# Cosine attention and a GELU layer on one core: q and k prepared over four slots, idle matmuls in the first batch

## Chip, cores and metric

One Trainium2 chip, one of its cores. The metric is the device time of one execution in microseconds (us), the median of several runs. Engines are named as in the profile: PE (TensorE, matmuls; PEld is its loading of weights), DVE (VectorE), ACT (ScalarE), POOL (GpSimd), SP (SyncE, here only a queue that issues DMAs).

## The reference

```python
# q, k, v: (8, 12, 448, 64); tau = 0.1
q_n = q / (norm(q, axis=-1) + 1e-06)
k_n = k / (norm(k, axis=-1) + 1e-06)
scores = q_n @ k_n.T / tau
attn = softmax(scores)
a = attn @ v                                   # (8, 12, 448, 64)
x = a.transpose(0, 2, 1, 3).reshape(8 * 448, 768)
h = x @ w_in                                   # w_in: (768, 2048)
g = 0.5 * h * (1 + erf(h / sqrt(2)))
out = g @ w_out                                # w_out: (2048, 768), out (3584, 768) f32
```

## The kernel before, in words

The 12 heads of a batch are taken as 6 pairs; the 48 pairs of all batches are numbered g = 0 to 47. For each pair the work is a row of steps, each a small function:

- `load_qk(g)` brings q and k of the pair (SP's queue, two DMAs), `load_v(g)` v (POOL's queue, cast to bf16).
- `square(g)` makes `sq` (1024 elements per partition) on POOL, `reduce(g)` the sums `nq` on DVE, `root(g)` the square root on ACT as Ln and Exp of half of it (`lq`, `sr`), `scale(g)` adds 1e-6 (`se`), takes the reciprocal (`rn`) on DVE and multiplies into `qkb`, q on POOL and k on DVE at the same time.
- `transposes(g)` puts `qkb` through PE into the bank `tp`, and DVE copies it out as `qkT`. `tp` shares its PSUM bank (tag "sm") with the sums `sm` of `values`.
- `scores(g, c0)` makes two of the four score tiles `st` on PE (two buffers) and their exponentials `pt` on ACT. The maximum isn't subtracted, since cosine scores are bounded.
- `values(g)` makes `sm` (sums of the exponentials, against ones) and `o` (against v) on PE, `normalise(g)` the reciprocal of the sums as Ln and Exp on ACT (`ln`, `rs`) and the product `x` on DVE.

`attention(b, fill)` runs a batch in six slots, one per pair. In slot g the kernel takes the scores of g, the values of g-1, the transposes of g+1 and the preparation of later pairs. Between them `run` puts in matmuls of `fill`: the second layer (`op`, 16 matmuls and a copy `ot` each) of the batches before, 96 of them in odd batches and 128 in even ones, none in batch 0. `first(b)` is the first layer of the batch (`hp`, 16 groups of 6 matmuls) with GELU on ACT (`g`); near its end it takes the transposes and the first half of the scores of the next batch's first pair. What is left of `op` comes at the end.

Each engine works its queue in the order in which the code is written (`manual_schedule`); an instruction that waits holds up what stands behind it. How far ahead a step runs is set by `upto(what, n, f)`, which calls f for all pairs up to n-1 that aren't done. The weights are loaded on POOL's queue (`wi` in 6 pieces, `wo` in 4), one or two per slot of batch 0.

The line numbers in the profile of before are those of the printed functions: `square` L103 to L106, `reduce` L113 and L115, `root` L121 and L123, `scale` L129 to L135, `transposes` L146 and L147, `scores` L157 and L160, `values` L170, `normalise` L178 to L181, `op` L196, `ot` L200, `hp` L289, GELU L293.

Of the kernel before, what the change touches and what calls it, by code (L numbers as in the profile page):

```python
# [8 lines left out]
F32 = mybir.dt.float32  # L9
BF16 = mybir.dt.bfloat16  # L10
AF = mybir.ActivationFunctionType
# [4 lines left out]
def kernel(  # L16
# [15 lines left out]
    nc = tc.nc  # L32
    B, H, S, D = q.shape
    NC = 4
    CS = S // NC
# [4 lines left out]
    KD = d_model // 128  # L40
# [3 lines left out]

    consts = ctx.enter_context(tc.tile_pool(name="consts", bufs=1))
    wpool = ctx.enter_context(tc.tile_pool(name="wpool", bufs=1))
    qkp = ctx.enter_context(tc.tile_pool(name="qkp", bufs=5))
    sqp = ctx.enter_context(tc.tile_pool(name="sqp", bufs=2))
    vp = ctx.enter_context(tc.tile_pool(name="vp", bufs=6))
    nrm = ctx.enter_context(tc.tile_pool(name="nrm", bufs=3))  # L50
    qkbp = ctx.enter_context(tc.tile_pool(name="qkbp", bufs=3))
# [8 lines left out]
    ps_mm = ctx.enter_context(tc.tile_pool(name="ps_mm", bufs=2, space=bass.MemoryType.PSUM))  # L60
# [3 lines left out]
    ident = consts.tile([CS, CS], BF16)  # L64
# [2 lines left out]
    nc.vector.memset(ones, 1.0)  # L67
    tiny = consts.tile([CS, 1], F32)
    nc.vector.memset(tiny, 1e-30)

    wi = wpool.tile([128, KD, d_ff], BF16, tag="wi")
    wo = wpool.tile([128, KF, d_model], BF16, tag="wo")
# [5 lines left out]
    x_t, g_t = {}, {}  # L78
# [19 lines left out]
    def square(g):  # L98
        sq = sqp.tile([CS, 2, 2, NC, D], F32, tag="sq", name=f"sq{g}")
        sq_t[g] = sq  # L100
        t = qk_t[g]
        if g == 0:
            nc.scalar.activation(sq[:, 1], t[:, 1], AF.Square)  # L103
            nc.vector.tensor_tensor(sq[:, 0], t[:, 0], t[:, 0], ALU.mult)
        else:
            nc.gpsimd.tensor_tensor(sq, t, t, ALU.mult)  # L106

# [32 lines left out]
    def transposes(g):  # L140
        qkb = qkb_t.pop(g)
        tp = ps_acc.tile([128, 2, NC, CS], BF16, tag="sm", name=f"tp{g}")
        qkT = qkTp.tile([128, 2, NC, CS], BF16, tag="qkT", name=f"qkT{g}")
        for i in (1, 0):
            for c in range(NC):
                nc.tensor.transpose(tp[:, i, c, :], qkb[:, i, c].rearrange("p h d -> p (h d)"), ident)  # L146
        nc.vector.tensor_copy(qkT, tp)  # L147
        qkT_t[g] = qkT


    def scores(g, c0):
        qkT = qkT_t[g]
        for c in (c0, c0 + 1):
            st = ps_st.tile([CS, 2, 512], F32, tag="st", name=f"st{g}_{c}")
            for h in range(2):
                rows = slice(h * D, (h + 1) * D)
                nc.tensor.matmul(st[:, h, :S], lhsT=qkT[rows, 1, c, :], rhs=qkT[rows, 0, :, :],  # L157
                                 start=True, stop=True)
            pt = ptp.tile([CS, 2, S], BF16, tag="pt", name=f"pt{g}_{c}")
            nc.scalar.activation(pt, st[:, :, :S], AF.Exp, scale=inv_tau)  # L160
            pt_t[g, c] = pt
# [65 lines left out]
    def upto(what, n, f):  # L227
        while done[what] < min(n, NG):
            f(done[what])
            done[what] += 1  # L230


    def attention(b, fill):
        fill = list(fill)

        def run(n):
            for _ in range(max(0, min(n, len(fill)))):
                fill.pop(0)()

        x_t[b] = xp.tile([128, HP, S], BF16, tag="x", name=f"x{b}")  # L240
        tail = 20 if fill else 0
        for i in range(HP):
            g = b * HP + i
            share = (len(fill) - tail) // (HP - i) if i else 30
            upto("red", g + 3 if g else 2, reduce)
            if g == 0 or i > 0:
                scores(g, 0)
            if i > 0:
                run(share // 3)
                upto("root", g + 3, root)  # L250
                values(g - 1)
                normalise(g - 1)
            else:
                run(24)
                upto("root", g + 3 if g else 2, root)
            if g == 0:
                upto("sc", 2, scale)
            scores(g, 2)
            if i < HP - 1:
                transposes(g + 1)  # L260
            if g == 0:
                upto("sq", 3, square)
                upto("red", 3, reduce)
                upto("root", 3, root)
            upto("sc", g + 3, scale)
            upto("sq", g + 4, square)
            upto("qk", g + 8, load_qk)
            upto("v", g + 4, load_v)
            for _ in range(2 if b == 0 and i < 4 else 1):
                if weights:  # L270
                    weights.pop(0)()
            run(share - share // 3 if i else 6)
        g = b * HP + HP - 1
        run(len(fill) - 8)
        values(g)
        normalise(g)
        run(len(fill))


    def first(b):  # L280
        sb, hf = divmod(b, 2)
        if hf == 0:
            g_t[sb] = gp.tile([128, KF, 2 * S], BF16, tag="g", name=f"g{sb}")
        nc.scalar.preload_act_table_set(GELU_SET)
        hps = {}

        def mm(m, kds):
            for kd in kds:
                nc.tensor.matmul(hps[m][:, :S], lhsT=wi[:, kd, m * 128:(m + 1) * 128],  # L289
                                 rhs=x_t[b][:, kd, :], start=(kd == 0), stop=(kd == KD - 1))  # L290

        def gelu(m):
            nc.scalar.activation(g_t[sb][:, m, hf * S:(hf + 1) * S], hps.pop(m)[:, :S], AF.Gelu)  # L293

        for m in range(KF):
            if m == KF - 5 and b + 1 < B:
                transposes((b + 1) * HP)
            if m != 1:
                hps[m] = ps_mm.tile([128, 512], F32, tag="mm", name=f"hp{b}_{m}")
            if m == 0:  # L300
                hps[1] = ps_mm.tile([128, 512], F32, tag="mm", name=f"hp{b}_1")
                mm(0, range(KD - 1))
                mm(1, range(KD - 1))
                mm(0, (KD - 1,))
            else:
                mm(m, (KD - 1,) if m == 1 else range(KD))
            gelu(m)
        if b + 1 < B:
            nc.scalar.preload_act_table_set(EXP_SET)
            scores((b + 1) * HP, 0)  # L310
# [1 line left out]

    upto("qk", 1, load_qk)
    nc.scalar.preload_act_table_set(EXP_SET)
    upto("qk", 5, load_qk)
    upto("v", 3, load_v)
    upto("sq", 1, square)
    upto("red", 1, reduce)
    upto("sq", 2, square)
    upto("root", 1, root)  # L320
    upto("sc", 1, scale)
    transposes(0)

    fill = []
    for b in range(B):
        attention(b, fill)
        first(b)
        sb, hf = divmod(b, 2)
        fill = [f for t in (range(3) if hf == 0 else range(3, 7)) for f in second_pieces(sb, t)]
# [37 lines left out]
```

## Time and profile before

| | |
|---|---|
| runs | 583.62, 584.01 and 586.18 us, median 584.01 |
| profiled execution | 584.36 us, of which the span of the profile is 582.6 |
| busy share of the span | PE 84%, ACT 56%, DVE 34%, POOL 34%, PEld 43% |
| granted TensorE clock, mean | 0.945 |
| moved by DMA | 45.35 MB |
| most expensive groups | `pt` on ACT 164.9 us (192), `op` 175.6 (896) and `hp` 150.0 (768) on PE |

Busy PE is modelled, since matmuls overlap in the pipeline; a share of 84% doesn't say that PE could do no more. In a row of the windows view stand the stretch (us from the start of the span), its length, for each engine the busy time and the instructions begun, the granted clock, the share of time that the 16 DMA engines were busy, and what they moved. In the chain of waits stand start, length, engine, tile and line: the work that ended last, followed back from the last instruction. In a row of the timeline the bracket gives the idle time of the engine ahead of the instruction, and what ended it.

### The profile page before, as it was taken

What the parts mean: (1) busy time and instruction counts of PE and PEld (TensorE: products, weight loads), DVE (VectorE), ACT (ScalarE), POOL (GpSimd) and SP (SyncE); (2) the same over time, 40 slices, a digit from 0 to 9 for tenths busy, and PEclk for the clock granted to TensorE, in tenths of its full rate; (3) what the DMA queues carried; (4) which work ended last, traced back from release to release, by engine and by line L of the source; (5) the groups of instructions that cost most, each with busy time, mean ns of one, the idle gap of its engine ahead of it and who ended that gap; (6) DMA issues with size and microseconds to landing.
All of it is one profiled execution on the core that took longest, in us unless ns stands there. A gap on an engine that the chain in (4) does not pass through costs nothing.

```text
span 582.6 us, 7930 instructions
## 1 busy us (share of the span) xinstructions
PE 492.1 (84%) x3200; PEld 248.1 (43%) x3200; DVE 195.6 (34%) x348; ACT 324.7 (56%) x529; POOL 196.3 (34%) x159
## 2 busy tenths in 40 slices
PE   2576997789987998779987999779988899869996
PEld 0233453345533454334543445334544455434453
DVE  4434114450255312443145412444124431453011
ACT  3465555664665546565565646556466655667410
POOL 4667305441144502543044420455025430440000
PEclk9996798899989999899998999789998899899999
DMA  8499903232044401324024420433114330110012
GB/s 213 105 199 200 198 2 100 58 96 67 3 104 108 121 13 40 92 64 125 1 68 106 107 66 1 107 79 104 31 37 101 80 97 1 37 16 28 28 27 82
DMA packets 42054, 45.35 MB, mean 78 GB/s; under 512 B 3361, under 2 KB 37665, under 8 KB 42017
## 3 DMA queue, kind: packets, MB, share of 16 engines
q1 hardware_dynamic: 27280, 32.81, 18.7%
q0 software_dynamic: 14496, 11.80, 14.3%
q8 instruction: 25, 0.41, 0.3%
q10 hardware_dynamic: 240, 0.23, 0.1%
q14 instruction: 13, 0.10, 0.1%
HBM read 45.61 MB, written 11.01 MB: 97 GB/s over the span
## 4 chain that ended last, share of the span: by engine, by line
PE 49%; POOL 20%; DVE 16%; ACT 9%; issue 4%; DMA 1%; POOLq 0%; SPq 0%
PE hp L289 25%; PE op L196 15%; POOL sq L106 12%; POOL qkb L135 9%; DVE nq L115 7%; DVE qkT L147 3%; DVE x L181 3%; PE tp L146 3%; ACT ln L178 3%; PE st L157 2%; ACT lq L121 2%; PE o L170 2%; ACT rs L180 2%; PE sm L170 2%; DVE rn L131 2%
## 5 line engine op out<-in xcount | busy, mean ns | idle before, releaser
L160 ACT ACTIVATE pt<-st 112x896 bf16<-112x896 f32 x192 | 164.9, 910 | 34.0 <-PE st L157 33.4
L135 POOL TENSOR_TENSOR qkb<-qk,rn 112x512 bf16<-112x512 f32 x48 | 70.3, 1464 | 324.4 <-DVE rn L131 284.7
L196 PE MATMUL op<-wo,g 128*128 128x384 bf16 x896 | 175.6, 346 | 0.0
L289 PE MATMUL hp<-x,wi 128*128 128x448 bf16 x768 | 150.0, 354 | 3.5 <-ACT g L293 3.5
L293 ACT ACTIVATE g<-hp 128x448 bf16<-128x448 f32 x128 | 68.8, 544 | 86.5 <-PE hp L289 86.5
L196 PEld LDWEIGHTS <-g 128*128 128x128 bf16 x896 | 85.2, 102 | 70.8 <-issue 28.2
L289 PEld LDWEIGHTS <-wi 128*128 128x128 bf16 x768 | 74.9, 98 | 74.6 <-issue 7.4
L115 DVE TENSOR_REDUCE nq<-sq 112x16 f32<-112x1024 f32 x47 | 57.3, 1218 | 103.3 <-POOL sq L106 103.3
L106 POOL TENSOR_TENSOR sq<-qk 112x1024 f32<-112x1024 f32 x47 | 88.6, 1885 | 2.8 <-DMA qk<-in_k_dram 2.8
L146 PE MATMUL tp<-ident,qkb 112*128 112x112 bf16 x384 | 30.1, 226 | 69.3 <-ACT ln L178 58.2
L157 PE MATMUL st<-qkT 64*112 64x448 bf16 x384 | 65.7, 413 | 9.1 <-DVE qkT L147 8.0
L121 ACT ACTIVATE lq<-nq,tiny 112x16 f32<-112x16 f32 x48 | 14.8, 308 | 96.8 <-DVE nq L115 95.7
L147 DVE COPY qkT<-tp 128x896 bf16<-128x896 bf16 x48 | 29.7, 618 | 106.4 <-PE tp L146 106.4
L200 DVE COPY ot<-op 128x384 f32<-128x384 f32 x56 | 31.0, 553 | 89.0 <-PE op L196 89.0
L146 PEld LDWEIGHTS <-qkb 112*128 112x128 bf16 x384 | 24.7, 103 | 84.7 <-issue 70.0
L170 PE MATMUL sm<-pt,ones 112*64 112x448 bf16 x384 | 53.2, 396 | 3.8 <-ACT pt L160 2.8
L181 DVE TENSOR_TENSOR x<-o,rs 128x448 bf16<-128x448 f32 x48 | 30.0, 625 | 73.4 <-ACT rs L180 48.5
L170 PE MATMUL o<-pt,v 112*64 112x448 bf16 x384 | 48.7, 379 | 0.0
L157 PEld LDWEIGHTS <-qkT 64*112 64x112 bf16 x384 | 22.2, 136 | 49.9 <-issue 28.0
L135 DVE TENSOR_TENSOR qkb<-qk,rn 112x512 bf16<-112x512 f32 x48 | 34.1, 710 | 1.8 <-DVE rn L131 0.2
L95 POOL DMA_DIRECT2D v<-in_v_dram x48 | 34.2, 712 | 0.2 <-issue 0.2
L170 PEld LDWEIGHTS <-ones 112*64 112x64 bf16 x384 | 19.8, 118 | 32.8 <-issue 27.0
(22 smaller groups left out, 139.1 us busy)
## 6 DMA issues: line engine op xcount, KB each, us to landing
qk<-in_q_dram SPq DMA_DIRECT2D x48, 224.0 KB, 2.8
qk<-in_k_dram SPq DMA_DIRECT2D x47, 224.0 KB, 3.0
v<-in_v_dram POOLq DMA_DIRECT2D x48, 112.0 KB, 3.0
wi<-in_moe_w_in_dram POOLq DMA_DIRECT2D x6, 512.0 KB, 6.7
wo<-in_moe_w_out_dram POOLq DMA_DIRECT2D x4, 768.0 KB, 11.7
out_dram<-ot SPq DMA_DIRECT2D x8, 336.0 KB, 2.9
out_dram<-ot SPq DMA_DIRECT2D x8, 288.0 KB, 2.6
out_dram<-ot SPq DMA_DIRECT2D x8, 240.0 KB, 3.1
```

Of the source, the lines that this page charges most:

```text
L106: nc.gpsimd.tensor_tensor(sq, t, t, ALU.mult)
L115: nc.vector.tensor_reduce(nq, sq, mybir.AxisListType.X, ALU.add)
L135: eng.tensor_tensor(qkb[:, i].rearrange("p c h d -> p h c d"), t[:, i], rn[:, i].to_broadcast([CS, 2, NC, D]), ALU.mult)
L146: nc.tensor.transpose(tp[:, i, c, :], qkb[:, i, c].rearrange("p h d -> p (h d)"), ident)
L147: nc.vector.tensor_copy(qkT, tp)
L157: nc.tensor.matmul(st[:, h, :S], lhsT=qkT[rows, 1, c, :], rhs=qkT[rows, 0, :, :], start=True, stop=True)
L160: nc.scalar.activation(pt, st[:, :, :S], AF.Exp, scale=inv_tau)
L170: nc.tensor.matmul(dst[h * D:(h + 1) * D, :S], lhsT=ones if dst is sm else v_t[g][:, h, c, :], rhs=pt_t[g, c][:, h, :], start=(c == 0), st ...
L181: nc.vector.tensor_tensor(x_t[b][:, p, :], o[:, :S], rs, ALU.mult)
L196: nc.tensor.matmul(ps[:, :NH], lhsT=g_t[sb][:, kf, t * 128:(t + 1) * 128], rhs=wo[:, kf, ni * NH:(ni + 1) * NH], start=(kf == 0), stop=(kf ...
L289: nc.tensor.matmul(hps[m][:, :S], lhsT=wi[:, kd, m * 128:(m + 1) * 128], rhs=x_t[b][:, kd, :], start=(kd == 0), stop=(kd == KD - 1))
L293: nc.scalar.activation(g_t[sb][:, m, hf * S:(hf + 1) * S], hps.pop(m)[:, :S], AF.Gelu)
```

## The change

The order of the preparation is changed, and with it the number of buffers. In slot g, POOL now squares pair g+4 (before: g+3) ahead of its multiplication of pair g+2 (before: behind it), DVE reduces pair g+3 (before: g+2), ACT takes the root of g+2 as before, and the scaling is of g+2 as before. q and k have 6 buffers instead of 5 and are loaded one pair earlier, `sq` has 3 instead of 2. Pair 1 is squared on ACT.

In batch 0 each call of `run` puts in four matmuls of zeros whose result nobody reads (`spin`), 56 in all, and 24 more stand ahead of the first transposes. In `first` the groups of `hp` are written one after another; before, groups 0 and 1 took their first five matmuls each, then their last ones.

```diff
-    qkp = ctx.enter_context(tc.tile_pool(name="qkp", bufs=5))
-    sqp = ctx.enter_context(tc.tile_pool(name="sqp", bufs=2))
+    qkp = ctx.enter_context(tc.tile_pool(name="qkp", bufs=6))
+    sqp = ctx.enter_context(tc.tile_pool(name="sqp", bufs=3))
...
+    blank = consts.tile([CS, S], BF16)
+    nc.vector.memset(blank, 0.0)
...
+        elif g == 1:
+            nc.scalar.activation(sq, t, AF.Square)
...
+    def spin(n):
+        ps = ps_mm.tile([128, 512], F32, tag="mm", name="spin")
+        for _ in range(n):
+            nc.tensor.matmul(ps[:CS, :S], lhsT=ident, rhs=blank, start=True, stop=True)
...
         def run(n):
+            if b == 0:
+                spin(4)
             for _ in range(max(0, min(n, len(fill)))):
                 fill.pop(0)()
...
-            upto("red", g + 3 if g else 2, reduce)
             if g == 0 or i > 0:
                 scores(g, 0)
+            upto("sq", g + 5, square)
+            upto("red", g + 4, reduce)
...
             scores(g, 2)
             if i < HP - 1:
                 transposes(g + 1)
-            if g == 0:
-                upto("sq", 3, square)
-                upto("red", 3, reduce)
-                upto("root", 3, root)
+            upto("root", g + 3, root)
             upto("sc", g + 3, scale)
-            upto("sq", g + 4, square)
-            upto("qk", g + 8, load_qk)
+            upto("qk", g + 9, load_qk)
...
         for m in range(KF):
             if m == KF - 5 and b + 1 < B:
                 transposes((b + 1) * HP)
-            if m != 1:
-                hps[m] = ps_mm.tile([128, 512], F32, tag="mm", name=f"hp{b}_{m}")
-            if m == 0:
-                hps[1] = ps_mm.tile([128, 512], F32, tag="mm", name=f"hp{b}_1")
-                mm(0, range(KD - 1))
-                mm(1, range(KD - 1))
-                mm(0, (KD - 1,))
-            else:
-                mm(m, (KD - 1,) if m == 1 else range(KD))
-            gelu(m)
+            hp = ps_mm.tile([128, 512], F32, tag="mm", name=f"hp{b}_{m}")
+            for kd in range(KD):
+                nc.tensor.matmul(hp[:, :S], lhsT=wi[:, kd, m * 128:(m + 1) * 128],
+                                 rhs=x_t[b][:, kd, :], start=(kd == 0), stop=(kd == KD - 1))
+            nc.scalar.activation(g_t[sb][:, m, hf * S:(hf + 1) * S], hp[:, :S], AF.Gelu)
...
-    upto("qk", 5, load_qk)
+    upto("qk", 6, load_qk)
     upto("v", 3, load_v)
+    spin(24)
     upto("sq", 1, square)
     upto("red", 1, reduce)
+    upto("root", 1, root)
     upto("sq", 2, square)
-    upto("root", 1, root)
     upto("sc", 1, scale)
     transposes(0)
+    upto("red", 2, reduce)
+    upto("sq", 4, square)
```

What the change makes of the order, at three places. The number behind a name is the pair's. POOL in batch 3, slots of pairs 19 and 20, before:

```order
L135 TENSOR_TENSOR qkb21_2357<-qk21_1723,rn21_2355 112x2x4x64
L106 TENSOR_TENSOR sq22_2360<-qk22_1817 112x1024
L95 DMA v22_2365<-in_v_dram 112x2x256
L135 TENSOR_TENSOR qkb22_2440<-qk22_1817,rn22_2438 112x2x4x64
L106 TENSOR_TENSOR sq23_2443<-qk23_1909 112x1024
L95 DMA v23_2448<-in_v_dram 112x2x256
```

and after (slots of pairs 20 and 21):

```order
L110 TENSOR_TENSOR sq24_2487<-qk24_2013 112x1024
L139 TENSOR_TENSOR qkb22_2546<-qk22_1827,rn22_2544 112x2x4x64
L97 DMA v23_2552<-in_v_dram 112x2x256
L110 TENSOR_TENSOR sq25_2571<-qk25_2097 112x1024
L139 TENSOR_TENSOR qkb23_2631<-qk23_1921,rn23_2629 112x2x4x64
L97 DMA v24_2637<-in_v_dram 112x2x256
```

The square that follows qkb of pair 22 was that of pair 23, and is now that of pair 25.

DVE in the slots of pairs 19 and 20, before:

```order
L147 COPY qkT20_2343<-tp20_2342 128x896
L129 TENSOR_SCALAR se21_2353<-sr21_2307 112x16
L131 RECIPROCAL rn21_2355<-se21_2353 112x16
L135 TENSOR_TENSOR qkb21_2357<-qk21_1723,rn21_2355 112x2x4x64
L115 TENSOR_REDUCE nq22_2373<-sq22_2360 112x16
L181 TENSOR_TENSOR x3_2209<-o19_2392,rs19_2412 128x448
L147 COPY qkT21_2426<-tp21_2425 128x896
```

and after:

```order
L151 COPY qkT20_2449<-tp20_2448 128x896
L133 TENSOR_SCALAR se21_2459<-sr21_2413 112x16
L135 RECIPROCAL rn21_2461<-se21_2459 112x16
L139 TENSOR_TENSOR qkb21_2463<-qk21_1736,rn21_2461 112x2x4x64
L119 TENSOR_REDUCE nq23_2489<-sq23_2399 112x16
L185 TENSOR_TENSOR x3_2313<-o19_2498,rs19_2518 128x448
L151 COPY qkT21_2532<-tp21_2531 128x896
```

The reduction between qkb of pair 21 and x of pair 19 was that of pair 22, whose square is behind qkb of pair 21 on POOL, and is now that of pair 23, whose square stands ahead of that qkb.

POOL at the start of batch 0, before:

```order
L106 TENSOR_TENSOR sq1_144<-qk1_120 112x1024
L135 TENSOR_TENSOR qkb0_154<-qk0_116,rn0_152 112x2x4x64
L135 TENSOR_TENSOR qkb1_189<-qk1_120,rn1_187 112x2x4x64
L106 TENSOR_TENSOR sq2_213<-qk2_123 112x1024
L135 TENSOR_TENSOR qkb2_225<-qk2_123,rn2_223 112x2x4x64
L106 TENSOR_TENSOR sq3_228<-qk3_126 112x1024
L95 DMA v3_239<-in_v_dram 112x2x256
L215 DMA wi_114<-in_moe_w_in_dram 128x2048 x2
```

and after:

```order
L139 TENSOR_TENSOR qkb0_184<-qk0_118,rn0_182 112x2x4x64
L110 TENSOR_TENSOR sq2_200<-qk2_125 112x1024
L110 TENSOR_TENSOR sq3_202<-qk3_128 112x1024
L110 TENSOR_TENSOR sq4_215<-qk4_131 112x1024
L139 TENSOR_TENSOR qkb1_234<-qk1_122,rn1_232 112x2x4x64
L139 TENSOR_TENSOR qkb2_266<-qk2_125,rn2_264 112x2x4x64
L97 DMA v3_278<-in_v_dram 112x2x256
L219 DMA wi_116<-in_moe_w_in_dram 128x2048 x2
```

sq of pair 1 is gone from POOL, and sq of pairs 2 to 4 stands ahead of qkb of pair 1.

More of the change, by code (lines that the diff above doesn't have):

```diff
@@ L284, in first @@
         nc.scalar.preload_act_table_set(GELU_SET)
[L285 to L293, printed above, removed]
         for m in range(KF):
```

## The prediction

> **What bounds the kernel now.** I read the page first: how busy each engine is, and the chain of work that ended last.
>
> ```profile
> span 582.6 us, 7930 instructions
> ## 1 busy us (share of the span) xinstructions
> PE 492.1 (84%) x3200; PEld 248.1 (43%) x3200; DVE 195.6 (34%) x348; ACT 324.7 (56%) x529; POOL 196.3 (34%) x159
> ...
> PE 49%; POOL 20%; DVE 16%; ACT 9%; issue 4%; DMA 1%; POOLq 0%; SPq 0%
> ```
>
> TensorE holds only half of the chain; over a third belongs to POOL and DVE, each busy a third of the time. So some stages are bound by a chain, not by an engine. The busy times by stretch tell which:
>
> ```profile
> core 0: us, PE busy (x) PEld busy (x) DVE busy (x) ACT busy (x) POOL busy (x), PEclk, DMA share, GB/s
> 20.14:62.45 42.31, 28.52 (x158) 12.53 (x154) 17.60 (x32) 25.67 (x44) 28.08 (x26) 0.82 0.95 186
> 24.80:72.20 47.40, 35.05 (x188) 16.12 (x188) 16.55 (x30) 28.19 (x47) 26.36 (x26) 0.82 1.02 198
> 36.75:44.68 7.93, 5.35 (x36) 2.46 (x33) 3.41 (x7) 4.87 (x8) 5.10 (x6) 0.96 1.01 196
> 62.45:83.22 20.77, 20.33 (x110) 10.16 (x108) 2.38 (x3) 9.53 (x17) 2.27 (x3) 0.95 0.48 91
> 221.00:269.38 48.38, 37.55 (x279) 18.64 (x278) 21.18 (x39) 31.71 (x51) 22.98 (x17) 0.96 0.32 78
> 243.15:251.07 7.92, 6.10 (x45) 2.69 (x42) 3.87 (x8) 4.93 (x9) 3.99 (x4) 0.86 0.35 74
> 269.38:289.06 19.68, 19.24 (x110) 9.83 (x108) 2.31 (x3) 8.87 (x17) 0.96 (x2) 1.00 0.17 46
> 289.06:337.49 48.43, 41.56 (x309) 21.53 (x310) 22.10 (x41) 31.64 (x51) 23.10 (x17) 0.96 0.36 87
> 557.05:582.60 25.55, 20.80 (x129) 12.33 (x126) 4.46 (x8) 0.54 (x1) 0.00 (x0) 0.95 0.23 62
> ```
>
> The first row is five slots of batch 0 and its end, the next but one a single slot in it, then `first(0)`; 221 to 269 is the attention of batch 3 with 96 `op` matmuls of filling, 243 to 251 a slot of it, 269 to 289 its `first`, 289 to 337 the attention of batch 4 with 128, the last row the end. `first` is TensorE's own (19.24 of 19.68 at a clock of 1.00). A slot is nobody's: 7.92 us, with PE 6.10, ACT 4.93, POOL 3.99, DVE 3.87. Batch 3 with 96 and batch 4 with 128 matmuls take the same 48.4 us, so the length of a slot isn't set by TensorE's work. The chain through that slot names what sets it:
>
> ```profile
> 243.15 1.45 POOL qkb L135
> 244.59 1.86 POOL sq L106
> ...
> 246.48 1.23 DVE nq L115
> ...
> 249.36 0.63 DVE x L181
> 249.99 0.53 DVE qkT L147
> 250.52 0.09 DVE se L129
> ...
> 251.07 1.45 POOL qkb L135
> ```
>
> It is a ring: POOL squares pair g+1 only behind qkb of pair g, DVE reduces it, ACT takes the root (behind it ln of the pair before, which frees the bank for tp), DVE does x, qkT, se, rn, and only then POOL has its next qkb. One lap is a slot.
>
> **The ring is cut.** With sq three, nq two, and root and scale one slot apart, nq(g+3) reads a square that POOL finished a slot earlier, lq(g+2) a reduction from the slot before, and transposes a qkb from the slot before. None waits within the slot. No instruction of a slot is added: sq, nq, lq, sr, se, rn, qkb, the v load and the two q and k loads stay one set per slot. POOL's 3.99 and DVE's 3.87 then hide under ACT's 4.93 or PE. The price is one more lap of distance in buffers (qk 6, sq 3). The q and k load on SP's queue still comes right behind the qkb that frees its buffer, and is used four slots later; those loads take a few us, so nothing there is late.
>
> What is late next? ACT with 4.93 per slot, or TensorE. Its prices at full clock, from the chain of waits in two places:
>
> ```profile
> 83.30 4.01 PE op L196 x24
> 87.30 0.52 PE st L157 x4
> 87.82 0.51 PE tp L146 x8
> ...
> 192.36 0.88 PE sm L170 x8
> 193.24 0.76 PE o L170 x8
> ```
>
> So an `op` matmul is 4.01/24 = 0.167, a slot's attention 2 x 0.52 + 0.51 + 0.88 + 0.76 = 3.19. With 9 `op` per slot (odd batches: 96 less 30 in slot 0 and 20 held back, over 5) PE needs 4.7, less than ACT's 4.93. With 15 or 16 (even batches, 128) it needs 5.8, more than ACT.
> - Odd attention: slot 0 has 30 `op`, two st and a tp: 5.01 + 0.52 + 0.51 = 6.05. Slots 1 to 4 by ACT: 4 x 4.93 = 19.7. Then slot 5 and the end on PE: half of st 0.26, 3 `op` 0.5, sm and o 1.64, st 0.52, 7 + 12 `op` 3.17, sm and o 1.64, 8 `op` 1.34, together 9.1. Sum 34.9, against 48.4.
> - Even attention: 6.05 + 4 x 5.8 + 0.26 + 28 `op` 4.68 + 1.64 + 0.52 + 1.64 + 1.34 = 39.3, against 48.4.
>
> Handing over between engines costs something that no row of before shows in this order. Its bounds are 0 and 1.2 us per slot (what se has lost beside sq, below). I take 0.2 for each of 6 slots, near the lower end, because only a single set of hand-overs per slot (rs, x, qkT, st, pt) lies in ACT's own rhythm: 36.1 and 40.5.
>
> **Batch 0.** There is no `op` to fill with; ACT's work in the stretch from 20.14 to 62.45 is 25.67 of 42.31. TensorE loses its clock there (0.82):
>
> ```profile
> 26.54 0.90 PE L146 MATMUL tp<-ident,qkb 112*128 112x112 bf16 x8 [3.62 <-ACT ln L178]
> 28.34 1.04 PE L157 MATMUL st<-qkT 64*112 64x448 bf16 x4 [0.90 <-DVE qkT L147]
> ```
>
> After 3.62 us of idling tp takes 0.90 instead of 0.51 and st 1.04 instead of 0.52. Four idle matmuls in each `run`, 8 per slot, 56 in the batch, 24 ahead of it. A spin streams 448 columns as `hp` does: (19.24 less 0.52 and 0.51)/96 = 0.19. Eight are 1.5 us, and PE's slot 3.19 + 1.5 = 4.7, still under ACT's 4.93; at half clock it would be 9.4. The 24 at the start lie in front of tp(0), where PE has nothing else: 4.6 us, or 9 if all are cold. They begin at about 1.5 us and tp(0) is wanted behind se, rn and qkb of pair 0, about 8.2; so they cost between 0 and 2.5, and I take 0, since the first cold ones are soon followed by warm ones.
>
> At the start sq(1) goes from POOL to ACT, which waits there anyway, so the step is hidden; and it uncovers something:
>
> ```profile
> 4.68 0.63 ACT L103 ACTIVATE sq<-qk 112x512 f32<-112x512 f32 x1 [2.21 <-DMA qk<-in_k_dram]
> ...
> 6.43 1.89 POOL L106 TENSOR_TENSOR sq<-qk 112x1024 f32<-112x1024 f32 x1 [2.81 <-DMA qk<-in_k_dram]
> 6.45 0.31 ACT L121 ACTIVATE lq<-nq,tiny 112x16 f32<-112x16 f32 x1 [1.14 <-DVE nq L113]
> 6.79 0.22 ACT L123 ACTIVATE sr<-lq 112x16 f32<-112x16 f32 x1
> 7.04 1.31 DVE L129 TENSOR_SCALAR se<-sr 112x16 f32<-112x16 f32 x1 [0.62 <-ACT sr L123]
> ```
>
> se of 16 elements takes 1.31 us here, and ends as POOL's sq does; in the quoted slot the step from se to rn is 0.1. So the first pair gains up to 1.2, of which I take 1.1. The Trainium skill, SBUF — State Buffer, section "Who interferes with whom", says that whichever of a DVE operation in a two-port mode, or with two SBUF inputs, and a GpSimd operation starts first keeps a shared port for its whole length and the other fully blocks; this row agrees (1.31 us, over when sq is). By that rule the change has a price, since sq now runs beside DVE's se and qkb in any slot where their times meet, while before the ring kept them apart; if a meeting fell in each slot the sum would be some 25 us longer; the same mechanism, priced by the row, stands among the rivals.
>
> POOL has 5.10 of work per slot with two weight loads (row 36.75), over ACT's 4.93, and its squares and qkb are in one queue with them: I take 1 us for the batch. The end behind the last exponential (last sm, o, four spins) is 1.5. So the stretch becomes 25.67 + 1.5 + 1 + 5 x 0.2 = 29.2, and `first(0)` starts at 62.45 - 42.31 + 29.2 - 1.1 = 48.2.
>
> **The transfers** are what could be late there: between 24.80 and 72.20 they ran full (share 1.02) at 198 GB/s, 47.4 us, mostly the weights. The first weights went out at 24.8; on POOL the same work stands ahead of them after the change, less sq(1) and the waits of the ring, some 3 us by an estimate, so they end near 69. wi is the first half, done by 46, and wanted at 48.2. The last quarter of wo is wanted 12 `op` into the filling of batch 1, at 48.2 + 19.5 + 2 = 69.7. It just fits; I take 1 us, between 0 and 5.
>
> **`first`** gets its groups one after another. That removes a wait:
>
> ```profile
> PE hp L289 <- ACT g L293: 3.5, 8, 0.4
> ```
>
> 0.4 each (in total, times, longest): hp of group 2 waited for gelu of group 0, which the split order had started late. The split covered a late x, but no wait of hp for x is among the waits, and o, 8 `op` and five `hp` (0.76 + 1.34 + 0.95 = 3.1) will still lie between the last sm and the first use of the last x (0.63 on DVE, behind two operations of ACT), so nothing comes in place of it. `first` is 19.24; `first(0)`, warm, 19.5 with what is cold at its beginning; the last, without tp and st, 18.3.
>
> **Sum.** 48.2 + 19.5 + 4 x 36.1 + 3 x 40.5 + 6 x 19.24 + 18.3 + 25.55 + 1 (wo) = 493.9. The profiled execution took 584.36 for its span of 582.6, and the median of the runs is 584.01, so I add 1.8: 496.
>
> **Rivals.**
> 1. *The loop without slack.* In ACT-bound slots x, qkT, st, two exponentials, lq to rs make a loop as long as ACT's own 4.93, and DVE's other work (nq, the ot copies, se held up by sq) can slip in ahead of x. For it: the 1.31 us se. Against: POOL is free half of the slot. At 1.2 us (1.31 less the usual 0.1) in 4 x 4 + 5 slots it is 25: 521. Chance 0.13.
> 2. *The spins don't hold the clock*, so the change doesn't do what it says in batch 0: 8.8 to 9.4 us per slot, longer than the 7.93 now. Five slots at 4 more: 516. Against: PE would then be busy throughout, and dense stretches are granted 1.00. Chance 0.06.
> 3. *Late weights*: wi stops `first(0)` or wo batch 1, up to 8 us in all: 503. Chance 0.10.
> 4. *Slower*: a denser stream is granted a lower clock. TensorE's work at full clock is 768 x 0.19 + 896 x 0.167 + 48 x 3.19 = 449; with 20 us of start and end it reaches 582 where the clock falls below 0.8 throughout; at 0.78 it gives 596. Against: 1.00 in the `first` row. Chance 0.02.
> 5. *Another wait closes a ring of the same length*, about 582; I find none in the order. Chance 0.02.
>
> **How the numbers follow.** The forecast has 0.67: 496, on its own 482 to 510 (no hand-over cost at one end, 0.5 a slot at the other). The range must take in rivals 1 to 3: 480 to 523. 0.5% (3 us) is what a measurement of this kernel can tell from no change; all but rivals 4 and 5 are faster: 0.96, same 0.02, slower 0.02.
>
> **What would show it.** Right: slots of 5.0 to 5.3 us in batch 0 and odd batches, about 5.9 in even ones; DVE's wait for sq gone, POOL's squares off the chain; ACT's share of the chain up; clock near 1.00 in batch 0; no wait of hp for g. Wrong: se or qkb on DVE of over 1 us in most slots (rival 1), tp of 0.9 and spins of 0.38 in batch 0 (2), PE waiting for wi or wo (3), clock under 0.8 in `first` (4). Most of the gain lies in seven batches of slots; if those stay near 7.9, the whole reading of the ring is wrong.

## The result, and the profile after

| | before | after |
|---|---|---|
| median of the runs, us | 583.82 (582.54 to 586.18, 4 runs) | 489.17 (488.45 to 489.69, 4 runs) |
| profiled execution, its span, us | 584.36, 582.6 | 489.69, 487.9 |
| granted clock, mean | 0.945 | 0.993 |
| moved by DMA, MB | 45.35 | 45.35 |

The changed kernel takes 0.8374 of the time before, with a 95% interval of 0.8345 to 0.8404. The forecast of 496 us was 7 too high and its range, 480 to 523, holds the result. Two later comparisons of the same pair gave ratios of 0.8379 and 0.836.

First the page of the changed kernel: span, busy times, and the chain of waits by engine.

```profile
span 487.9 us, 8097 instructions
...
PE 474.8 (97%) x3280; PEld 245.2 (50%) x3280; DVE 198.5 (41%) x349; ACT 323.1 (66%) x530; POOL 195.8 (40%) x158
...
PE 88%; DMA 4%; ACT 3%; DVE 2%; POOL 1%; issue 1%; SPq 1%; POOLq 0%
```

POOL, DVE and ACT do nearly the same work as before (195.8, 198.5 and 323.1 us). What went is the time in which they waited for each other. TensorE holds 88% of the chain, where it held 49%, and POOL fell from 20% to 1%.

The windows of the changed kernel, with the columns of before: `first(0)`, the attention of batch 1, one slot of it, `first(1)`, the attention of batch 2, one slot of it, the end, the later part of batch 0, and one slot of that.

```profile
49.88:69.42 19.54, 19.39 (x110) 9.93 (x109) 2.95 (x4) 9.64 (x17) 3.45 (x4) 1.00 1.03 200
69.42:104.78 35.36, 35.26 (x278) 17.88 (x278) 20.82 (x39) 31.07 (x51) 24.14 (x18) 1.00 0.48 120
84.30:89.19 4.89, 4.89 (x43) 2.40 (x41) 3.70 (x8) 4.68 (x9) 4.04 (x4) 1.00 0.53 110
104.78:123.85 19.07, 19.07 (x109) 9.84 (x108) 2.31 (x3) 8.97 (x17) 0.00 (x0) 1.00 0.08 23
123.85:163.52 39.67, 39.67 (x309) 20.53 (x310) 22.03 (x41) 31.07 (x51) 24.12 (x18) 1.00 0.46 118
139.68:145.39 5.71, 5.71 (x48) 2.87 (x47) 3.87 (x8) 4.76 (x9) 4.02 (x3) 1.00 0.42 84
462.33:487.90 25.57, 20.80 (x129) 12.33 (x126) 4.46 (x8) 0.54 (x1) 0.00 (x0) 1.00 0.22 62
20.00:49.88 29.88, 29.82 (x219) 14.50 (x218) 22.48 (x31) 25.96 (x43) 26.30 (x25) 0.94 1.01 210
26.80:31.87 5.07, 5.06 (x42) 2.54 (x41) 3.36 (x7) 4.92 (x9) 4.61 (x5) 1.00 0.97 192
```

A slot takes 4.89 us in an odd batch and 5.71 in an even one; before, it took 7.92, and both kinds of batch 48.4. The two kinds now differ by their `op` matmuls, so TensorE's work sets the length. POOL's 4.04 and DVE's 3.70 lie inside it. In the slot of batch 0 TensorE is the fullest engine too (5.06 of 5.07), with the idle matmuls counted in. The chain of waits through the odd slot (start, length, engine, tile, line) has one engine left; its first three pieces, behind which sm, o, st and tp follow:

```profile
84.30 0.98 PE op L200 x6
85.28 0.67 PE st L161 x4
85.94 0.59 PE op L200 x3
```

The longest of TensorE's waits in the changed kernel (who waited, for what: us in total, times, longest):

```profile
PE tp L150 <- DVE qkb L139: 4.4, 1, 4.4
```

It is 4.4 us at the start, for the second pair; no other is over 1.3. In the first slots of batch 1 the chain still runs through ACT and DVE (75.8 to 80.2 us), but in its whole attention TensorE is idle for only 0.10 us of 35.36. None of `hp` for GELU or of TensorE for weights is left.

### The profile page after: what moved, and what is told of

It reads as the page before. It is cut to its first block, busy times and chain, and to the rows that moved or that the text cites. A ratio compares the mean times of both kernels' runs of the same rounds, so it can differ in the third digit from the quotient of the medians.

```text
span 487.9 us, 8097 instructions
## 1 busy us (share of the span) xinstructions
PE 474.8 (97%) x3280; PEld 245.2 (50%) x3280; DVE 198.5 (41%) x349; ACT 323.1 (66%) x530; POOL 195.8 (40%) x158
## 2 busy tenths in 40 slices
DMA packets 42053, 45.35 MB, mean 93 GB/s; under 512 B 3360, under 2 KB 37664, under 8 KB 42016
## 4 chain that ended last, share of the span: by engine, by line
PE 88%; DMA 4%; ACT 3%; DVE 2%; POOL 1%; issue 1%; SPq 1%; POOLq 0%
PE op L200 30%; PE hp L299 30%; PE st L161 10%; PE sm L174 7%; PE o L174 6%; PE tp L150 4%; DMA qk<-in_k_dram 4%; ACT pt L164 2%; PE spin L240 1%; DVE x L185 1%; POOL qkb L139 1%; SPq L89 1%; ACT rs L184 1%; DVE qkT L151 1%; ACT ln L182 0%
## 5 line engine op out<-in xcount | busy, mean ns | idle before, releaser
L200 PE MATMUL op<-wo,g 128*128 128x384 bf16 x896 | 161.3, 326 | 0.0
L301 ACT ACTIVATE g<-hp 128x448 bf16<-128x448 f32 x128 | 69.6, 544 | 80.2 <-PE hp L299 80.2
L200 PEld LDWEIGHTS <-g 128*128 128x128 bf16 x896 | 81.2, 98 | 62.4 <-issue 15.9
L161 PE MATMUL st<-qkT 64*112 64x448 bf16 x384 | 60.7, 376 | 1.6 <-DVE qkT L151 0.7
L174 PE MATMUL sm<-pt,ones 112*64 112x448 bf16 x384 | 45.8, 360 | 0.0
L174 PE MATMUL o<-pt,v 112*64 112x448 bf16 x384 | 44.3, 352 | 0.0
L161 PEld LDWEIGHTS <-qkT 64*112 64x112 bf16 x384 | 20.5, 125 | 39.3 <-issue 28.1
L182 ACT ACTIVATE ln<-sm 128x448 f32<-128x448 f32 x48 | 25.5, 532 | 21.3 <-PE sm L174 21.2
L139 DVE TENSOR_TENSOR qkb<-qk,rn 112x512 bf16<-112x512 f32 x48 | 37.1, 773 | 1.9 <-DMA qk<-in_k_dram 0.2
L150 PE MATMUL tp<-ident,qkb 112*128 112x112 bf16 x384 | 27.9, 215 | 5.3 <-DVE qkb L139 4.4
L150 PEld LDWEIGHTS <-qkb 112*128 112x128 bf16 x384 | 20.5, 98 | 20.7 <-issue 13.2
L174 PEld LDWEIGHTS <-ones 112*64 112x64 bf16 x384 | 17.7, 109 | 23.1 <-issue 15.9
```

The source lines that it names most:

```text
L139: eng.tensor_tensor(qkb[:, i].rearrange("p c h d -> p h c d"), t[:, i], rn[:, i].to_broadcast([CS, 2, NC, D]), ALU.mult)
L174: nc.tensor.matmul(dst[h * D:(h + 1) * D, :S], lhsT=ones if dst is sm else v_t[g][:, h, c, :], rhs=pt_t[g, c][:, h, :], start=(c == 0), st ...
L200: nc.tensor.matmul(ps[:, :NH], lhsT=g_t[sb][:, kf, t * 128:(t + 1) * 128], rhs=wo[:, kf, ni * NH:(ni + 1) * NH], start=(kf == 0), stop=(kf ...
L301: nc.scalar.activation(g_t[sb][:, m, hf * S:(hf + 1) * S], hp[:, :S], AF.Gelu)
```

## Experiments

Times are medians. Kernels compared with each other ran on the same chip wherever possible. Where they didn't, I go by each one's ratio to the kernel before on its own chip.

### One link of the ring cut, and nothing else

The kernel before, with the square one pair further ahead. Root and scaling stay where they were, and there are no idle matmuls.

```diff
-    sqp = ctx.enter_context(tc.tile_pool(name="sqp", bufs=2))
+    sqp = ctx.enter_context(tc.tile_pool(name="sqp", bufs=3))
...
-            upto("sq", g + 4, square)
+            upto("sq", g + 5, square)
```

> The kernel before with one thing changed: POOL squares pair g+4 instead of g+3 behind its qkb in slot g, with three sq buffers instead of two. Theory (a ring, cut by its cheapest link): nq no longer waits for a square of the same lap. What remains as a loop through DVE's own order is nq 1.22, lq and sr 0.54, ln 0.44, rs 0.59, x 0.62, qkT 0.53, se and rn 0.36, qkb on DVE 0.69, hand-overs 0.3: 5.3 us. So slots of about 5.3 in batch 0 and the odd batches, 5.7 to 5.9 in the even ones, 497 to 507 us in all (the 489 of the change, 8 for 21 slots of 5.3 instead of 4.9, 3 for the wait of hp for gelu, a few for batch 0 without idle matmuls). Rival (all of the preparation has to be spread): the lap only loses the square, 1.9 of 7.9, slots of 6.0 in odd and even batches alike, 515 to 522. Second rival (the ring wasn't the bound): above 570.

Measured: 500.03 us (499.52 to 501.0), ratio 0.8553 (0.8522 to 0.8583). One lap of its chain in an odd batch, from one reduction to the next:

```profile
83.89 1.14 DVE nq L115
...
86.68 0.62 DVE x L181
...
88.24 0.69 DVE qkb L135
88.93 0.47 DVE ot L200
89.40 1.14 DVE nq L115
```

POOL is off the chain, and the lap takes 5.51 us instead of 7.92. What is left is a shorter ring of DVE and ACT (root, ln and rs lie on ACT between the first two pieces), because the reduction still stands ahead of the root in the same slot. So this one link is worth 84 of the 95 us, within the 497 to 507 that I had expected.

The other 10 us (spans of 497.9 and 487.9) don't come mainly from that shorter ring. These are the attention of batches 1 and 2 in this kernel:

```profile
72.03:108.24 36.21, 35.63 (x277) 17.95 (x278) 20.73 (x39) 31.52 (x51) 23.77 (x18) 1.00 0.46 115
127.91:167.60 39.69, 39.69 (x310) 20.54 (x310) 22.04 (x41) 31.10 (x51) 23.76 (x18) 1.00 0.48 118
```

An odd attention is 0.85 us longer than in the changed kernel (36.21 against 35.36), about 3 us in four batches, since the chain goes through DVE and ACT only until 93 us and then stays on TensorE. An even one is the same (39.69 against 39.67). `first`, which has its old order here, takes 19.67 in batch 1 instead of 19.07, between 4 and 5 us in eight batches, and `first(0)` begins 2.4 later (52.31 against 49.88).

### Idle matmuls alone

The kernel before, with the 56 and the 24 idle matmuls and nothing else.

```diff
         def run(n):
+            if b == 0:
+                spin(4)
...
+    spin(24)
```

> The kernel before with the idle matmuls alone: four in each run of batch 0 and 24 at the start. Ring theory: TensorE's links in batch 0's lap are short, so a full clock shortens nothing there, slots stay at 7.9 us; only the start and the first hp of first(0) gain, 0 to 2 us: 581 to 584. Rival (batch 0 is slow because TensorE is cold): its five slots go to 6 to 7 us, 574 to 578.

Measured: 583.17 us (580.87 to 584.62, 10 runs), ratio 0.9978 (0.9957 to 0.9998). Two slots of batch 0, one behind the other, from one qkb of POOL in the chain of waits to the next, and TensorE's timeline there (start, length, engine, line, tile; in brackets the idle time ahead of it):

```profile
28.15:36.03 7.88, 7.73 (x44) 3.29 (x41) 3.37 (x7) 4.92 (x9) 5.05 (x6) 0.64 1.03 208
36.03:43.96 7.93, 5.16 (x42) 2.62 (x41) 3.41 (x7) 4.87 (x9) 5.11 (x6) 1.00 1.01 204
```

```profile
25.82 0.55 PE L148 MATMUL tp<-ident,qkb 112*128 112x112 bf16 x8 [3.71 <-ACT ln L180]
...
28.59 1.74 PE L238 MATMUL spin<-blank,ident 112*112 112x448 bf16 x4
30.27 1.70 PE L172 MATMUL sm<-pt,ones 112*64 112x448 bf16 x8
...
37.19 0.95 PE L172 MATMUL sm<-pt,ones 112*64 112x448 bf16 x8
```

The slots still take 7.9 us. In the first of them TensorE runs at half rate (sm 1.70), in the second at full rate (sm 0.95, 5.16 busy instead of 7.73), and the second is no shorter. So in batch 0 too it was the ring and not the clock that set them. Nor do eight idle matmuls hold the clock in every such slot: behind the gap of 3.71 us four of them take 1.74 instead of 0.92.

### The changed kernel without idle matmuls

Both calls of `spin` are taken out.

```diff
-            if b == 0:
-                spin(4)
...
-    spin(24)
```

> The changed kernel without any idle matmul. Theory (they hold the clock, which matters once the ring is cut): TensorE's 3.2 us of work per slot at full clock become 6.2 at half, more than ACT's 4.9, so batch 0's slots go from 5.07 to 6.0 or more and first(0) starts 4 to 7 us later and cold: 493 to 497. Rival (short slots keep TensorE busy enough by themselves): slots of 5.1, 488 to 490. Second rival (the idle matmuls get in the way): 486 to 488.

Measured: 488.43 us (488.02 to 491.38), ratio 0.8363 (0.8326 to 0.84). The idle matmuls bring nothing that can be measured, and my own theory (493 to 497) fell. The windows of two of its slots in batch 0, then TensorE's timeline from the second of them into the next slot:

```profile
19.59:25.85 6.26, 5.54 (x33) 2.22 (x34) 3.41 (x7) 4.69 (x8) 5.23 (x5) 1.00 0.79 197
...
30.74:36.53 5.79, 5.05 (x33) 2.17 (x34) 4.15 (x7) 4.99 (x9) 5.29 (x6) 0.71 1.01 196
```

```profile
30.74 0.93 PE L161 MATMUL st<-qkT 64*112 64x448 bf16 x4 [1.25 <-DVE qkT L151]
31.59 1.71 PE L174 MATMUL sm<-pt,ones 112*64 112x448 bf16 x8
...
37.27 0.95 PE L174 MATMUL sm<-pt,ones 112*64 112x448 bf16 x8
```

In these two slots TensorE runs at half rate (sm 1.71), and they take 6.26 and 5.79 us; the slot behind each has sm at 0.95 and takes 4.89, and the fifth is at full rate too (sm 0.95). With idle matmuls sm takes 0.95 from the second slot on, so they do hold the clock once the ring is cut. But they cost what they save. With them the scores of 25.85, 30.74, 36.53 and 41.42 stand at 26.80, 31.87, 36.94 and 42.01: slots of 5.07 against 5.19 on average, behind a start that is 0.9 later. TensorE reaches `hp` at 47.80, 2.1 us earlier than in the changed kernel's first trace, and then finds the last x missing:

```profile
47.80 1.12 PE L297 MATMUL hp<-x,wi 128*128 128x448 bf16 x5
...
50.51 0.61 DVE L185 TENSOR_TENSOR x<-o,rs 128x448 bf16<-128x448 f32 x1
...
51.17 5.06 PE L297 MATMUL hp<-x,wi 128*128 128x448 bf16 x17 [2.25 <-DVE x L185]
```

That x comes no earlier than with idle matmuls (50.47 in the changed kernel), although ACT's rs had ended at 48.30: ahead of it on DVE stand a se of 2.72 us and a qkb of 1.54. So in this execution it is DVE that lets `first(0)` begin. The profiled execution is the slowest of the four (491.38): behind the wait `hp` ran slow for a while, 0.30 each instead of 0.19. The other three took 488.0 to 488.6; I have no trace of them.

### The old order of `first`

The changed kernel with groups 0 and 1 of `hp` split as before.

```diff
-            for kd in range(KD):
-                nc.tensor.matmul(hp[:, :S], ...)
+            if m == 0:
+                mm(0, range(KD - 1))
+                mm(1, range(KD - 1))
+                mm(0, (KD - 1,))
+            else:
+                mm(m, (KD - 1,) if m == 1 else range(KD))
```

> The changed kernel with the order of hp of before (groups 0 and 1 take five matmuls each, then their last). Theory (hp of group 2 waits for a gelu that the split started late): 0.4 us per batch come back in each of eight first layers, 492 to 493, with 8 waits of PE hp for ACT g, 3.5 us in all. Rival (the split covers a late x, which the faster slots could bring back): equal or up to 1 us faster than 489, most likely in first(0), where hp waited for the last x.

Measured: 492.61 us (492.09 to 493.18), ratio 0.8421 (0.8387 to 0.8455). Its waits have the row of before again:

```profile
PE hp L298 <- ACT g L302: 3.5, 8, 0.4
```

Eight waits of 0.44 are 3.5 us. The medians differ by 3.4 from the first comparison's 489.17, the ratios by 0.0047, or 2.7 us.

### What batch 0 loses: the order at the start

POOL squares pairs 3 and 4 only behind qkb of pair 1, where the changed kernel has them ahead of it.

```diff
-            upto("sq", g + 5, square)
-            upto("red", g + 4, reduce)
+            if g == 0:
+                upto("red", 2, reduce)
+            else:
+                upto("sq", g + 5, square)
+                upto("red", g + 4, reduce)
...
-    upto("sq", 4, square)
+    upto("sq", 3, square)
```

(The steps left out in slot 0 follow behind its transposes: squares to pair 3 ahead of root and scaling, pair 4 behind them.)

> The changed kernel with another order at the start only: qkb of pair 1 on POOL ahead of the squares of pairs 3 and 4 (in the change behind them), and se of pair 1 on DVE ahead of the reductions of pairs 2 and 3. Theory (the change made its own start late: POOL was in the squares of pairs 3 and 4 from 12.7 to 16.5 us, and qkb of pair 1 ended at 18.4): the first exponential of pair 1, at 21.1 now, comes at 17.5 to 19, and the whole rest as much earlier: 486 to 487.5. Rival (the weights' transfers, full until 60 us, hold first(0) back): start earlier, hp of first(0) at 50 as now, 489.

Measured: 488.43 us (488.25 to 488.53), ratio 0.8363 (0.8349 to 0.8377), against 489.43 (488.82 to 489.73) for the changed kernel on that chip. The start of the changed kernel, then of this one, from the timeline:

```profile
12.73 3.76 POOL L110 TENSOR_TENSOR sq<-qk 112x1024 f32<-112x1024 f32 x2 [0.46 <-DMA qk<-in_k_dram]
...
16.89 1.55 POOL L139 TENSOR_TENSOR qkb<-qk,rn 112x512 bf16<-112x512 f32 x1 [0.40 <-DVE rn L135]
...
21.14 1.73 ACT L164 ACTIVATE pt<-st 112x896 bf16<-112x896 f32 x2 [5.87 <-PE st L161]
```

```profile
17.90 1.71 ACT L164 ACTIVATE pt<-st 112x896 bf16<-112x896 f32 x2
```

POOL's qkb of pair 1 begins at 13.64 instead of 16.89, and the exponentials of pair 1 come 3.2 us earlier (2.6 against the changed kernel's trace from the same chip, where they begin at 20.55). Yet the kernel gains only 1.0, between the theory and the rival: the last x of batch 0 starts at 49.35 instead of 50.47 (50.45 on the same chip). The rest was lost on the way.

### What batch 0 loses: DVE and POOL at the same time

Where it goes, in the changed kernel's timeline near the end of batch 0:

```profile
42.20 1.92 POOL L110 TENSOR_TENSOR sq<-qk 112x1024 f32<-112x1024 f32 x1
...
42.52 3.75 DVE L139 TENSOR_TENSOR qkb<-qk,rn 112x512 bf16<-112x512 f32 x1
...
44.06 1.05 POOL L139 TENSOR_TENSOR qkb<-qk,rn 112x512 bf16<-112x512 f32 x1
...
45.04 0.72 POOL L97 DMA_DIRECT2D v<-in_v_dram  x1
...
49.01 0.58 ACT L184 ACTIVATE rs<-ln 128x448 f32<-128x448 f32 x1
49.03 1.52 DVE L139 TENSOR_TENSOR qkb<-qk,rn 112x512 bf16<-112x512 f32 x1 [0.24 <-DMA qk<-in_k_dram]
...
50.47 0.61 DVE L185 TENSOR_TENSOR x<-o,rs 128x448 bf16<-128x448 f32 x1
```

DVE's qkb, usually 0.69, takes 3.75: it lasts until POOL has done a square, its own qkb and a v load. The bracket of the second qkb names a load, and the chain of waits books 8.62 us on it, but this pair had been squared two slots earlier, so its k had long landed. Up to the last x se takes 4.24 us in 8 instructions (0.17 each without a meeting), and qkb of DVE 9.42 in 8 (0.69): together 6.8 us over. The last x itself starts 0.9 us behind the end of ACT's rs (49.59). In later batches it doesn't happen (se at most 0.26, qkb 0.69). There POOL no longer loads weights, 1.1 to 1.5 us per slot, ahead of its squares. So I moved the weight loads behind the square and ahead of qkb.

```diff
             upto("sq", g + 5, square)
+            if g > 0:
+                load_weights(i)
             upto("red", g + 4, reduce)
```

> The changed kernel with the weight loads of batch 0 issued on POOL behind the square and ahead of qkb, from slot 1 on (in the change behind qkb). Theory (port: two loads of 1.1 to 1.5 us behind qkb push the next square so late that it meets DVE's se and qkb, which then wait for POOL): the square starts 1.1 to 1.5 us earlier, se is back at 0.17 and qkb on DVE at 0.7 in slots 1 to 5, where they lost 6.5 us in all, the last x of batch 0 comes about 1 us earlier and hp of first(0) doesn't wait for it: 488 to 488.7. Rival (the transfer of k, which the chain of waits names ahead of that x): qkb on DVE and x as late as now, 489.2.

Measured: 490.6 us (490.29 to 491.83), ratio 0.8405 (0.8388 to 0.8421): 1.2 us slower than the changed kernel on that chip, and outside both the theory and the rival. As expected, se and qkb meet nothing in slots 1 to 4 (se 0.16 to 0.33). But in slot 5 this stands in the timeline:

```profile
46.62 0.81 POOL L223 DMA_DIRECT2D wo<-in_moe_w_out_dram  x1
...
47.23 4.40 DVE L139 TENSOR_TENSOR qkb<-qk,rn 112x512 bf16<-112x512 f32 x1 [0.22 <-DVE rn L135]
47.45 1.05 POOL L139 TENSOR_TENSOR qkb<-qk,rn 112x512 bf16<-112x512 f32 x1
...
48.44 0.72 POOL L97 DMA_DIRECT2D v<-in_v_dram  x1
...
49.17 1.91 POOL L110 TENSOR_TENSOR sq<-qk 112x1024 f32<-112x1024 f32 x1
...
51.56 0.61 DVE L185 TENSOR_TENSOR x<-o,rs 128x448 bf16<-128x448 f32 x1
```

One qkb of 4.40 us, right ahead of the last x, undoes all of it: that x starts 1.1 us later than in the changed kernel on that chip (50.45). It stood behind four POOL instructions in a row, the next slot's square included. A third kernel had both edits, v of the first three pairs loaded later, and no idle matmuls behind the last scores:

> Both of the above together, and the loads of v of pairs 0 to 2 behind the square of pair 2 so that q and k land earlier, and no idle matmuls behind the last scores of batch 0. Theory: start 3 us, end of batch 0 1 to 2 us, 484 to 486.5. Rival (transfers hold the end of batch 0): 488 to 489.

Measured: 490.45 us (489.72 to 491.23), ratio 0.8398 (0.8382 to 0.8415), again outside both, and again with a qkb of 4.39 ahead of x. What counts is not how many meetings there are, but whether one delays the last x.

### The last x first

The scaling in the last slot is for a pair of the next batch and can wait. The next kernel has the start order above, puts the scaling and the load of q and k in each batch's last slot behind the last normalise, and leaves out the idle matmuls behind the last scores.

```diff
-            upto("sc", g + 3, scale)
+            if i < HP - 1:
+                upto("sc", g + 3, scale)
...
         normalise(g)
+        upto("sc", g + 3, scale)
+        upto("qk", g + 9, load_qk)
```

> The start order of the run before, and in the last slot of each batch the scaling (se, rn, qkb) behind the last x instead of ahead of it, and no idle matmuls behind the last scores of batch 0. Theory (the last x of batch 0 stands on DVE behind a qkb that waits for POOL's port through two or three of POOL's instructions): x comes with ACT's rs, near 49.0 instead of 49.9, and hp doesn't wait for four idle matmuls: 487 to 487.7 against 488.4 for the start order alone and 489.4 for the change. Rival (it is the transfer of k): x as late as now, 488.2 to 488.6.

Measured: 489.21 us (488.86 to 490.22), ratio 0.8371 (0.8356 to 0.8386). The changed kernel on that chip took 488.76 (488.28 to 488.94), ratio 0.836, so this is outside both the theory and the rival, and no gain. Against the changed kernel's trace from that chip, x comes 1.5 us earlier (48.04 instead of 49.55) and batch 1 begins 1.4 earlier (67.11 instead of 68.50), but the end begins 0.6 later (461.94 instead of 461.37): 2.0 us were given back. The waits name half of that:

```profile
PE hp L314 <- DVE ot L204: 1.0, 6, 0.2
```

In later batches nothing had met there, and the scaling now holds up DVE's copies of `op` that `hp` waits for. The same edit on the third kernel of the section above:

> The run with all starts (weights ahead of qkb, v later, start order), with the scaling of each batch's last slot behind the last x. Theory: the qkb of 4.4 us no longer stands ahead of x, hp's third us of waiting goes: 490.45 falls by 2 to 3, to 487 to 488.5. Rival (something else made it slower than the start order alone): 489.5 to 490.5.

Measured: 489.0 us (487.64 to 490.43), ratio 0.8366 (0.8342 to 0.8389), with the same giving back. Its four runs took 490.43, 490.27, 487.64 and 487.72; the trace is of the first, and what made the last two faster is not known. So the scaling was moved in batch 0 alone:

```diff
-            upto("sc", g + 3, scale)
+            if b or i < HP - 1:
+                upto("sc", g + 3, scale)
```

> As the run with start order and scaling last, but the scaling stands behind the last x in batch 0 alone. Theory (the two edits gained 2.3 us up to the first op of batch 1, and each later batch gave 0.3 back, since hp then waited for an ot copy, six times, 1.0 us in all): the gain of 2.3 stays, 486.5 to 487.5, ratio near 0.834. Rival (the later batches' 0.3 us have another cause): 488.7 to 489.2.

Measured: 487.33 us (487.19 to 488.31, 5 runs), ratio 0.8344 (0.8324 to 0.8363). This is as the theory had it. Its timeline at the end of batch 0:

```profile
46.97 0.95 PE L174 MATMUL o<-pt,v 112*64 112x448 bf16 x8 [0.94 <-DVE x L185]
...
48.02 0.62 DVE L185 TENSOR_TENSOR x<-o,rs 128x448 bf16<-128x448 f32 x1 [1.11 <-PE o L174]
```

x comes 2.45 us earlier than in the first trace of the changed kernel, `op` of batch 1 begins 2.33 earlier (67.09) and the end begins 2.32 earlier (460.01 instead of 462.33). Against the trace whose x starts at 49.55 these are 1.5, 1.4 and 1.4. Over nine traces with the new order of `first` and TensorE warm there, `op` of batch 1 began 18.95 to 19.07 us behind the start of that x. A meeting still delays x here: o of the last pair waits 0.94 us for x of the pair before, since both need the one bank of o, and that x stands behind a qkb of 3.75. It is the fastest kernel of the study, by 1.4 to 2.1 us or 0.3 to 0.4% against three medians of the changed kernel on other chips. The interval of its ratio overlaps two of the changed kernel's three, so this is likely but not shown.

### The changed kernel again

The changed kernel ran along in two of these comparisons, unaltered.

> The changed kernel beside these three on the same chip, as their measure: 489, ratio 0.837.

> The changed kernel beside these two on the same chip, as their measure: 489.4, ratio 0.838.

Measured: 489.43 us, ratio 0.8379 (0.8365 to 0.8394), and 488.76, ratio 0.836 (0.8347 to 0.8374). These are the changed kernel's figures in the comparisons above; between chips its median differs by 0.7 us. In its three traces the last x of batch 0 starts at 50.47, 50.45 and 49.55, so between traces from different chips a shift of 1 us there doesn't tell two kernels apart.

## Why the prediction was right, and where it was not

The terms of the sum against the windows (from the start of `op` of one batch to the next for attention and `first` together):

| term, us | forecast | measured |
|---|---|---|
| until `hp` of `first(0)` | 48.2 | 49.88 |
| `first(0)` | 19.5 | 19.54 |
| odd attention and `first`, three times | 55.34 | 54.43 |
| even attention and `first`, three times | 59.74 | 58.74 |
| last odd attention and last `first` | 54.4 | 53.39 |
| end | 25.55 | 25.57 |
| wait for wo | 1 | 0 |
| sum | 493.9 | 487.9 |

**The ring** was read rightly. Cutting one link alone gave 84 of the 95 us, and idle matmuls without the cut gave 1 or none. All of it came from waits; POOL's and DVE's own work did not get shorter. Root and scaling of a pair stand in the same slot, not one apart as I wrote, but nothing waits for that: in the odd slot sr ends at 87.81 and the se that reads it begins at 89.96.

**The next bound** was right for even batches, where TensorE sets 5.7 us. For odd ones I had ACT's 4.93, from a slot of before. ACT takes 4.68 there now and TensorE 4.89, so both are nearly full, and TensorE ends last.

**The step that failed** is handing over: 0.2 us for each of six slots. It measured next to nothing. In the two slot rows TensorE is busy for the whole length (4.89 of 4.89, 5.71 of 5.71). There are always a few `op` between a result and its use, and the price of 0.2 was put between bounds that no row of before tied to this order. The row nearest to it was `first`, where TensorE also runs on filled gaps and loses next to nothing (19.24 of 19.68). At zero the attention would have been 34.9 and 39.3; it measured 35.36 and 39.67, of which TensorE is busy for 35.26 and 39.67, so what is over is its own work, taken some 0.4 too small. Seven attentions at 1.2 put 8.4 us too much into the sum. That it missed by 6 only is luck: the later start (1.7) and TensorE's own work (2.8) had been taken too small. Without any handing over the working gives 486.6 (496 less 8.4 and the 1.0 of batch 0), and not the 482 that I gave as its lower end. `first` was 0.17 shorter than its row of before.

**The start** had the wrong sign: `hp` begins 1.7 us later than forecast (0.8 in the trace where it begins at 48.95). se of pair 0 is freed as I said: in the changed kernel it takes 0.17 instead of 1.31. But I made the sum for pair 0 alone and took the 1.1 us through to the end. Pair 1 decides, and for it POOL's squares of pairs 3 and 4 now stand ahead of qkb, a row that I had shown in the order and not priced. Its exponentials begin at 21.14 (20.55 and 20.50 in the other two traces) instead of 20.14, and putting those squares behind brings 2.6 us there on one chip.

**The idle matmuls** I costed at nothing, as hidden behind the gain of a warm TensorE. The clock they hold (sm 0.95 in each slot but the first), but the gain is used up by their own time and the later start: with them TensorE itself fills the slots of batch 0 (5.06 of 5.07, ACT 4.92), and at the batch's end it is DVE's last x that `hp` needs. The row of before from which I took the loss of the clock doesn't show it either: sm took 1.71 at 18.79, so TensorE ran at half rate ahead of the 3.62 us of idling too. The Trainium skill, TensorE: Matmul & The Clock Gate, section "Part 1: The HAM clock gate", puts the fall to half rate behind an idle window of about 3.4 us. The trace with idle matmuls alone has one such fall (tp took 0.55 right after 3.71 idle, st 1.04 at 27.63). The kernel without idle matmuls doesn't agree: it fell to half rate at about 31 us, though it had not been idle for longer than 1.25 us at a stretch since 20 us.

**Rival 1** was half right. Its mechanism, DVE held up beside POOL, is there, but in batch 0 alone and not in the steady slots, where POOL's square ends before se begins, though only just. In the odd slot:

```profile
87.73 1.91 POOL L110 TENSOR_TENSOR sq<-qk 112x1024 f32<-112x1024 f32 x1
...
89.96 0.17 DVE L133 TENSOR_SCALAR se<-sr 112x16 f32<-112x16 f32 x1
```

The square ends at 89.64, 0.32 us ahead of se. My reason against the rival, that POOL is free half of the slot, came from a slot of 7.92; in one of 4.89 POOL works for 4.04. So that the steady slots were spared is partly luck. In batch 0 the meetings cost 6.8 us of DVE's time, which the slots mostly absorb; what they cost the kernel is part of the lateness of the last x. How much isn't separated: the last experiment's x comes 1.5 to 2.45 us earlier, of which the start order alone brings 1.1, and the rest came with two edits at once, the scaling behind x and no idle matmuls ahead of it. The Trainium skill, SBUF — State Buffer, section "Who interferes with whom", speaks of an exclusive lock for one instruction. The measurement is harsher: one qkb of 3.75 and one of 4.40 us waited through three and four POOL instructions in a row.

**Rivals 2 to 5.** Idle matmuls that don't hold the clock are seen where the ring is left in place, and not after the cut. TensorE never waited for weights. The clock was 1.00 in nearly all stages. No other ring closed.

Open is what the changed order would gain in batch 0 if DVE and POOL didn't meet at all: each move of the loads only moved the meetings, and a kernel without them wasn't tried.

## What to carry to other kernels

If no engine is busy for more than its share of a repeated slot, and slots with different loads take the same time, follow the chain for one lap: it names a ring. Find the link that is cheapest to take a slot ahead with one more buffer, and price the new slot as the fullest engine's work, without a surcharge for handing over as long as independent work lies between, as it did here. Read how full the other engines are from the new, shorter slot and not from the old one. Give the start a sum of its own by the second item, not the first, and look at what stands in the queue ahead of the last result that a stage waits for, since one collision there costs more than many elsewhere.

## What I had not expected of the hardware

- A DVE multiplication of 112x512 from two SBUF tiles took 4.40 us instead of 0.69. It had started 0.22 ahead of POOL's qkb, while POOL was issuing a DMA, and ended 0.55 us after POOL's fourth instruction from there. None of the short gaps between POOL's instructions let it in.
- An operation on 16 elements per partition (se) took up to 2.72 us beside POOL, against 0.17.
- Without idle matmuls TensorE fell back to half rate at about 31 us, behind a slot of 4.89 us with gaps of at most 1.25 us, and the granted clock of a window of a few us doesn't always tell it: 19.59 to 25.85 has 1.00, though sm took 1.71 there. The length of a matmul is the surer sign.
